# Opening a linear-attention and MLP kernel with a quarter of q loaded by another queue, and with a new order of transposes, sums and products

## Chip, cores and metric

One Trainium2 chip, one NeuronCore. The metric is the device time of one execution in microseconds (us). The kernel before takes 294.88 us, the median of 4 runs (294.63 to 294.96).

The engines, as the profile names them: PE (TensorE matmul), PEld (its weight loads), DVE (VectorE), ACT (ScalarE), POOL (GpSimd) and SP (SyncE, which here only issues DMAs). Each works through its own list of instructions in order and waits on semaphores. DMAs are issued by POOL (all input loads), by SP (output stores, small transfers through DRAM, transposing DMAs) and twice by ACT at the end.

## The reference

```python
# q, k, v: (8, 8, 576, 64) fp32; moe_w_in: (512, 2048); moe_w_out: (2048, 512)
phi = lambda x: np.where(x > 0, x, np.exp(x) - 1.0) + 1.0
q_p, k_p = phi(q), phi(k)
kv  = np.einsum('bhsd,bhse->bhde', k_p, v)
z   = np.sum(k_p, axis=2)
num = np.einsum('bhsd,bhde->bhse', q_p, kv)
den = np.einsum('bhsd,bhd->bhs', q_p, z)[..., None] + 1e-06
x   = (num / den).transpose(0, 2, 1, 3).reshape(4608, 512)
h   = x @ w_in
out = (h - np.tanh(h)) @ w_out
```

## The kernel before

**Layout.** A batch (8 heads of 576 positions) is loaded as four blocks of 128 partitions (8 heads by 64 position groups of J = 9 positions), and held as two halves i = 0, 1. phi (`phi_pieces`, L121) is an exp on ACT (`e`), a max/add on DVE (`r`) and a min on DVE, into `qp` and `kp`. qp is transposed to `qT`: for batches 0 and 1 by PE with copies out of PSUM by ACT or DVE (`a_qT_pe`, L157), for later batches by one transposing DMA on SP (`a_qT_dma`, L151). kv and z come from matmuls of kp with v and with ones (`a_kv` L180, `a_kv_cols` L191 with v repacked by `a_vp` L188; for batch 0 `b0_kv` L216 and `b0_z` L205). DVE multiplies them with a mask of the head blocks into `kz` (L186, L202, L214, L225). `a_den` (L267) multiplies qT with the z columns, DVE takes the reciprocal (L285).

**Spreading 1/den.** For batches 2 and later `a_spread` (L301) writes the reciprocals to DRAM (`ds`, four DMAs on SP) and reads them back on all partitions (`rdb`, two DMAs); `a_num` (L324) multiplies num by rdb into `xT` (L328, L333). For batch 1 the reciprocal is split into bf16 parts (`a_split` L288) and spread by matmuls (`a_spread_pe` L348, line L354), num having been copied from PSUM by ACT (`a_num_copy`, L341); `a_scale` (L359) multiplies. Batch 0 does the same in fp32 (`b0_spread` L235, `b0_num` L227, `b0_scale` L242), with its ninth positions by DRAM (`b0_rest`).

**The MLP.** The 4608 rows go in 9 chunks of 512 (the loop at L502). A chunk does 16 tiles of the first layer (`l1mm`, L366, 4 matmuls each), each pair of tiles followed by tanh on ACT (L372) and a subtraction on DVE (L373) into `gT`, and then 16 steps of 4 matmuls of the second layer (`l2mm`, L387); every fourth step ends a block of 128 rows, copied out by ACT (`evac`, L396) and stored by two DMAs on SP (L401). Chunk 0 has single tiles (`l1act`, L377, L378).

**What sets the order.** It is written out by hand: each engine gets its instructions in the order of the Python calls. Lists `s1[tile]` and `s2[step]` say what of the next batches is put behind which tile or step; this is where the attention work of batch n1 = c + 1 and the phi of batch n2 = c + 2 stand. For chunk 0 s2[3] to s2[15] hold phi of q, transposes, kv, den, num and spread of batch 1, and phi of q and k of batch 2. For chunk 1 kv_cols stands at tile 7 and den at tile 10. From chunk 1 on the loads of batch n2 wait for a small POOL copy (`gate`, L383) of the transposed q of batch n1: they are issued when that transposing DMA has landed.

**The opening** (L404 to L481). POOL issues the two halves of q, of k and of v of batch 0, then the weights and batch 1. PE runs 18 dummy matmuls (`spin`, L444) until the first half of qp is there, transposes it, 5 more, transposes the other half, 6 more, then z(0), kv(0), z(1), den, num(0), kv(1), the spread of two head pairs, num(1). ACT copies three of the four transposed pieces, DVE one. ACT's order is: exp of both q halves, one copy, exp of k half 0, exp of k half 1 in two, two copies, the four small casts `s8` (L460), `sel`, num.

**PSUM.** `ps_all` has 8 banks. The side work of chunk 0 takes banks 4 to 7 in turn, the first layer of later chunks banks 0 to 5, their attention work banks 6 and 7; a matmul that begins a bank waits for whoever last read it.

## Time and profile before

| | us |
|---|---|
| median of 4 runs | 294.88 |
| the profiled execution's own time | 295.09 |
| span of its instructions | 293.3 |
| PE busy | 286.0 |
| DVE busy | 174.7 |
| ACT busy | 139.6 |
| first matmul of the first layer (L366) | 16.70 |
| first layer of chunk 1 begins | 51.26 |
| second layer of chunk 1 begins | 67.25 |

Times in the timeline are from the start of the span. A timeline row is: start, length, engine, line, operation, output and input by the program's names, how many; in brackets the idle time of the engine before it and what ended that. The view of waits has, for each pair of a waiting and a releasing group: total us, times, longest us. Matmuls overlap in PE's pipeline (a 128x512 one shows 379 ns and the next starts 216 ns later), so holes on PE are read from the distance of starts, not from the busy share. A row of the DMA view has 40 equal slices of its window.

### The profile page before, as it was taken

How to read it: one execution, taken by the hardware profiler on the slowest of the kernel's cores; microseconds unless marked ns; L12 is line 12 of the kernel's file. 1: busy time of each engine (PE TensorE's matmuls, PEld its weight loads, DVE VectorE, ACT ScalarE, POOL GpSimd, SP SyncE). 2: the span in 40 equal slices, each digit the busy share in tenths (PEclk: the TensorE clock that was granted, in tenths of full speed). 3: DMA queues.
4: the chain of work that ended last, by engine and by line, in shares of the span. 5: the costliest groups of instructions: out<-in, count | busy, mean ns of one | idle time of the engine just before them, and what ended most of it. 6: DMA issues, size and time to landing. Idle time of an engine off the chain costs nothing.

```text
span 293.3 us, 4504 instructions
## 1 busy us (share of the span) xinstructions
PE 286.0 (98%) x1801; PEld 134.6 (46%) x1801; DVE 174.7 (60%) x265; ACT 139.6 (48%) x168; POOL 33.6 (11%) x55
## 2 busy tenths in 40 slices
PE   8999999999999999999999999999999999999994
PEld 3544453454444444544454444444444444444443
DVE  4759957887467764786478646865581456106600
ACT  4838537947344653455246524661452155126411
POOL 8583030030030003000300020000000000000000
PEclk9999999999999999999999999999999999999999
DMA  6999999998989758945895669767117310131032
GB/s 97 194 204 212 208 207 217 204 146 145 238 162 187 156 118 139 219 119 126 135 223 117 153 134 181 138 151 144 38 23 179 73 36 0 38 84 24 0 74 72
DMA packets 39077, 38.94 MB, mean 133 GB/s; under 512 B 16336, under 2 KB 33808, under 8 KB 38288
## 3 DMA queue, kind: packets, MB, share of 16 engines
q0 software_dynamic: 17552, 18.35, 38.7%
q1 hardware_dynamic: 21344, 20.17, 30.6%
q8 instruction: 14, 0.23, 0.3%
q10 hardware_dynamic: 160, 0.13, 0.1%
q14 instruction: 7, 0.06, 0.0%
HBM read 43.91 MB, written 9.55 MB: 182 GB/s over the span
## 4 chain that ended last, share of the span: by engine, by line
PE 70%; DMA 17%; issue 7%; POOL 2%; DVE 1%; ACT 1%; SPq 1%; POOLq 0%; DVEq 0%
PE ps_all L366 35%; PE ps_all L387 30%; DMA qraw<-in_q_dram 6%; DMA w_in_sb<-in_moe_w_in_dram 3%; DMA rdb<-ds 3%; PE ps_all L199 2%; DMA out_dram<-osb 2%; DMA kraw<-in_k_dram 2%; PE ps_all L317 2%; DMA ds<-rden 1%; PE ps_all L276 1%; ACT osb L396 1%; SPq L401 0%; POOL qraw L90 0%; ACT e L134 0%
## 5 line engine op out<-in xcount | busy, mean ns | idle before, releaser
L366 PE MATMUL ps_all<-xT,w_in_sb 128*128 128x512 bf16 x576 | 128.0, 379 | 0.3 <-DVE xT L244 0.3
L387 PE MATMUL ps_all<-w_out_sb,gT 128*128 128x512 bf16 x560 | 127.8, 379 | 0.0
L373 DVE TENSOR_TENSOR gT<-ps_all,th 128x1024 bf16<-128x1024 f32 x64 | 77.9, 1218 | 59.8 <-ACT th L372 59.8
L372 ACT ACTIVATE th<-ps_all 128x1024 f32<-128x1024 f32 x64 | 65.5, 1024 | 57.0 <-PE ps_all L366 47.1
L366 PEld LDWEIGHTS <-w_in_sb 128*128 128x128 bf16 x576 | 55.3, 98 | 66.6 <-issue 0.6
L387 PEld LDWEIGHTS <-gT 128*128 128x128 bf16 x560 | 54.0, 98 | 64.5 <-issue 0.5
L396 ACT COPY osb<-ps_all 128x512 f32<-128x512 f32 (+1 forms) x36 | 20.9, 582 | 73.7 <-PE ps_all L387 57.3
L328 DVE TENSOR_TENSOR xT<-ps_all,rdb 128x512 bf16<-128x512 f32 x24 | 16.3, 689 | 13.7 <-PE ps_all L317 11.2
L134 ACT ACTIVATE e<-qraw 128x1152 bf16<-128x1152 bf16 x16 | 18.5, 1162 | 6.6 <-DMA qraw<-in_q_dram 6.6
L134 ACT ACTIVATE e<-kraw 128x1152 bf16<-128x1152 bf16 x15 | 17.5, 1165 | 0.2 <-DMA kraw<-in_k_dram 0.2
L136 DVE TENSOR_TENSOR qp<-e,r 128x1152 bf16<-128x1152 bf16 x16 | 12.0, 757 | 7.7 <-ACT e L134 7.2
L136 DVE TENSOR_TENSOR kp<-e,r 128x1152 bf16<-128x1152 bf16 x15 | 11.4, 758 | 8.5 <-ACT e L134 7.6
L383 POOL COPY g<-qT 1x1 bf16<-1x1 bf16 x5 | 1.4, 273 | 120.8 <-DMA qT<-qp 120.8
L378 DVE TENSOR_TENSOR gT<-ps_all,th 128x512 bf16<-128x512 f32 x16 | 10.3, 685 | 2.4 <-ACT th L377 1.7
L377 ACT ACTIVATE th<-ps_all 128x512 f32<-128x512 f32 x16 | 9.2, 598 | 4.3 <-PE ps_all L366 3.1
L444 PE MATMUL ps_all<-zero 128*128 128x512 bf16 x29 | 9.6, 498 | 1.2 <-DVE zero L405 1.2
L317 PE MATMUL ps_all<-qT,kz 128*128 128x512 bf16 x28 | 10.1, 379 | 0.1
L135 DVE TENSOR_SCALAR r<-qraw 128x1152 bf16<-128x1152 bf16 x16 | 7.2, 453 | 2.1 <-DMA qraw<-in_q_dram 2.1
L199 PE MATMUL ps_all<-vp,kp 64*128 64x136 bf16 x216 | 7.4, 220 | 0.4 <-POOL g L383 0.4
L199 PEld LDWEIGHTS <-kp 64*128 64x128 bf16 x216 | 6.4, 94 | 3.0 <-issue 2.1
L285 DVE RECIPROCAL rden<-den 128x144 f32<-128x144 f32 x7 | 7.4, 1053 | 0.2
L394 DVE COPY osb<-ps_all 128x128 f32<-128x128 f32 x1 | 0.3, 290 | 11.6 <-DMA out_dram<-osb 11.6
(82 smaller groups left out, 122.1 us busy)
## 6 DMA issues: line engine op xcount, KB each, us to landing
out_dram<-osb SPq DMA_DIRECT2D x70, 128.0 KB
rdb<-ds SPq DMA_DIRECT2D x12, 576.0 KB
kraw<-in_k_dram POOLq DMA_DIRECT2D x7, 576.0 KB, 7.0
qraw<-in_q_dram POOLq DMA_DIRECT2D x7, 576.0 KB, 9.1
v<-in_v_dram POOLq DMA_DIRECT2D x7, 576.0 KB, 12.1
w_out_sb<-in_moe_w_out_dram POOLq DMA_DIRECT2D x4, 512.0 KB, 16.3
w_in_sb<-in_moe_w_in_dram POOLq DMA_DIRECT2D x6, 256.0 KB, 8.3
qraw<-in_q_dram POOLq DMA_DIRECT2D x2, 288.0 KB, 4.6
```

The lines of the kernel that those rows point to most:

```text
L134: return (lambda: nc.scalar.activation(e, x, AF.Exp), lambda: nc.vector.tensor_scalar(r, x, 0.0, 1.0, ALU.max, ALU.add), lambda: nc.vector ...
L136: lambda: nc.vector.tensor_tensor(y, e, r, ALU.min))
L199: nc.tensor.matmul(ps[hg][:, i, :], kp[r, i, j].rearrange("p h d -> p (h d)"), vp[r, i, j, :], start=(j == 0), stop=(j == J - 1))
L317: nc.tensor.matmul(ps, kz[:, p // 2, p % 2, 0:128], qT[:, p % 2, 0:8, p // 2, :], start=True, stop=True)
L328: nc.vector.tensor_mul(xT[:, p, S * b:S * b + 512].rearrange("p (j t c) -> p j t c", j=8, t=4), ps.rearrange("p j (t c) -> p j t c", t=4), ...
L366: nc.tensor.matmul(h, w_in_sb[:, 2 * (p % 2) + p // 2, fi * 128:(fi + 1) * 128], xT[:, p, c * 512:(c + 1) * 512], start=(n == 0), stop=(n ...
L372: nc.scalar.activation(th, h, AF.Tanh)
L373: nc.vector.tensor_sub(gT[:, fi:fi + 2, :], h, th)
L378: nc.vector.tensor_sub(gT[:, fi, :], h, th)
L387: nc.tensor.matmul(o, gT[:, fi, i * 128:(i + 1) * 128], w_out_sb[:, fi, :], start=(fi == 0), stop=(fi == NF - 1))
L396: nc.scalar.copy(osb[:, f0:f1], o[:, f0:f1])
L444: nc.tensor.matmul(ps_all[:, 0, :], zero[:, 0:128], zero, start=True, stop=True)
```

## The change

Seven edits in one diff, here by place:

- **Load of q, batch 0.** The first half of q was one POOL DMA with two blocks. Now block 0 goes by SP, as fp32, into memory that the pool of `gT` lends (`q_f`); block 1 goes by POOL. POOL's number of DMAs stays the same.
- **phi of that half** is done by block: exp, max/add and min each in two, of 128x576.
- **Order in the opening.** 14, 5 and 5 dummy matmuls instead of 18, 5 and 6. The four casts `s8` stand behind the first two exps. The copies of the transposes stand behind all exps of k: three on ACT, the fourth on DVE behind the mask of z(0). z(1) stands ahead of kv(0); the banks of z and kv are exchanged.
- **Batch 1 in chunk 0.** kv between the two sets of transposes rather than behind both; num right behind den, one step earlier, with the split of the reciprocal.
- **phi of batch 2.** Each piece of q one step later (steps 13, 14, 15 rather than 12, 13, 14), the last beside phi of k.
- **Chunk 1.** exp of k half 1 stays at tile 1, its max/add and min go to tile 3; vp half 1 stays on DVE at tile 3, half 0 goes to ACT at tile 5.
- **Chunk 1.** kv_cols at tile 9 rather than 7, den and its DRAM transfers at tile 11 rather than 10.

On ACT the copies out of PSUM of chunk 0's last two blocks thereby stand one place earlier against the exps, and on SP the transposing DMA of batch 2 stands behind all 8 output stores of chunk 0 rather than behind 6.

```diff
--- before.py
+++ after.py
@@ -87,6 +87,12 @@
         x = src[b].rearrange("h (p j) d -> (h p) (j d)", j=J)
         if halves:
             for i in range(2):
+                if src is q and i == 0:
+
+                    nc.sync.dma_start(out=q_f, in_=x.rearrange("(h i q) x -> h i q x", h=2, i=2)[0, 0])
+                    nc.gpsimd.dma_start(out=t[:, 1, i].rearrange("q j d -> q (j d)"),
+                                        in_=x.rearrange("(h i q) x -> h i q x", h=2, i=2)[1, 0])
+                    continue
                 nc.gpsimd.dma_start(out=t[:, :, i].rearrange("q h j d -> q h (j d)"),
                                     in_=x.rearrange("(h i q) x -> i q h x", h=2, i=2)[i])
         else:
@@ -118,7 +124,7 @@
 
     kp_t, qp_t, qT_t, kz_t, rdb_t, rden_t = {}, {}, {}, {}, {}, {}
 
-    def phi_pieces(b, src, store, name, i, parts=0):
+    def phi_pieces(b, src, store, name, i, xs=None):
 
         if i == 0:
             store[b] = work.tile([128, 2, J, 2, D], BF16, name=name)
@@ -126,11 +132,13 @@
         e = epool.tile([128, 2, J, D], BF16, name="e")
         r = epool.tile([128, 2, J, D], BF16, name="r")
         y = store[b][:, i].rearrange("p j h d -> p h j d")
-        if parts:
-
-            return ([lambda h=h: nc.scalar.activation(e[:, h], x[:, h], AF.Exp) for h in range(2)],
-                    lambda: nc.vector.tensor_scalar(r, x, 0.0, 1.0, ALU.max, ALU.add),
-                    [lambda h=h: nc.vector.tensor_tensor(y[:, h], e[:, h], r[:, h], ALU.min) for h in range(2)])
+        if xs:
+
+            return ([lambda h=h: nc.scalar.activation(e[:, h], xs[h], AF.Exp) for h in range(2)],
+                    [lambda h=h: nc.vector.tensor_scalar(r[:, h], xs[h], 0.0, 1.0, ALU.max, ALU.add)
+                     for h in range(2)],
+                    [lambda h=h: nc.vector.tensor_tensor(y[:, h], e[:, h], r[:, h], ALU.min) for h in range(2)],
+                    lambda: nc.vector.tensor_scalar(r, x, 0.0, 1.0, ALU.max, ALU.add))
         return (lambda: nc.scalar.activation(e, x, AF.Exp),
                 lambda: nc.vector.tensor_scalar(r, x, 0.0, 1.0, ALU.max, ALU.add),
                 lambda: nc.vector.tensor_tensor(y, e, r, ALU.min))
@@ -169,6 +177,18 @@
             else:
                 nc.vector.tensor_copy(dst, src)
 
+    def b0_T(i):
+
+        if i == 0:
+            new_qT(0)
+        src = []
+        for n, (j0, j1) in enumerate(((0, 5), (5, 9))):
+            ps = ps_all[:, 4 + 2 * i + n, :].bitcast(BF16).rearrange("p (j t) -> p j t", t=128)
+            for j in range(j0, j1):
+                nc.tensor.transpose(ps[:, j - j0, :], qp_t[0][:, i, j].rearrange("p h d -> p (h d)"), ident)
+            src.append((qT_t[0][:, i, j0:j1].rearrange("p j g t -> p j (g t)"), ps[:, 0:j1 - j0, :]))
+        return src
+
     def kv_mm(b, i, ps):
         kp, vt = kp_t[b], v_b[b % 2]
         for j in range(J):
@@ -187,6 +207,9 @@
 
     def a_vp(b, i):
         nc.vector.tensor_copy(vp[:, i, :, 0:128].rearrange("p j (h d) -> p h j d", h=2), v_b[b % 2][:, 0:2, i])
+
+    def a_vp_act(b, i):
+        nc.scalar.copy(vp[:, i, :, 0:128].rearrange("p j (h d) -> p h j d", h=2), v_b[b % 2][:, 0:2, i])
 
     def a_kv_cols(b, banks):
         kp = kp_t[b]
@@ -207,22 +230,22 @@
         for j in range(J):
             for hg in range(2):
                 r = slice(64 * hg, 64 * hg + 64)
-                nc.tensor.matmul(ps_all[:, 4 - 2 * i + hg, 0:32], kp_t[0][r, i, j].rearrange("p h d -> p (h d)"),
+                nc.tensor.matmul(ps_all[:, 2 - 2 * i + hg, 0:32], kp_t[0][r, i, j].rearrange("p h d -> p (h d)"),
                                  one[r, 0:32], start=(j == 0), stop=(j == J - 1))
 
     def b0_zc(i):
-        nc.vector.tensor_mul(kz_t[0][:, :, i, 128:160], ps_all[:, 4 - 2 * i:6 - 2 * i, 0:32], mask[:, :, i, 128:160])
+        nc.vector.tensor_mul(kz_t[0][:, :, i, 128:160], ps_all[:, 2 - 2 * i:4 - 2 * i, 0:32], mask[:, :, i, 128:160])
 
     def b0_kv(i):
 
         for j in range(J):
             for hg in range(2):
                 r = slice(64 * hg, 64 * hg + 64)
-                nc.tensor.matmul(ps_all[:, 2 * i + hg, 0:128], kp_t[0][r, i, j].rearrange("p h d -> p (h d)"),
+                nc.tensor.matmul(ps_all[:, 2 + hg, 0:128], kp_t[0][r, i, j].rearrange("p h d -> p (h d)"),
                                  v_b[0][r, 0:2, i, j, :], start=(j == 0), stop=(j == J - 1))
 
     def b0_kz(i):
-        nc.vector.tensor_mul(kz_t[0][:, :, i, 0:128], ps_all[:, 2 * i:2 * i + 2, 0:128], mask[:, :, i, 0:128])
+        nc.vector.tensor_mul(kz_t[0][:, :, i, 0:128], ps_all[:, 2:4, 0:128], mask[:, :, i, 0:128])
 
     def b0_num(i, ns):
 
@@ -405,6 +428,8 @@
     nc.vector.memset(zero, 0.0)
     act0 = rpool.tile([128, 1], F32, name="act0")
     nc.scalar.activation(act0, zero[:, 0:1], AF.Exp)
+
+    q_f = gpool.tile([128, NF, 512], BF16, name="gT").rearrange("p a b -> p (a b)").bitcast(F32)[:, 0:J * D]
     load_q(0)
     load_k(0)
     make_identity(nc, ident)
@@ -445,30 +470,39 @@
 
     side = Banks([4, 5, 6, 7])
     kz_t[0] = kz_c[0]
-    (eq0, rq0, mq0), (eq1, rq1, mq1) = (phi_pieces(0, q_t, qp_t, "qp", i) for i in range(2))
-    for f in (eq0, rq0, mq0, eq1, rq1, mq1):
+    q_h = [q_f.rearrange("p (j d) -> p j d", d=D), q_t[0][:, 1, 0]]
+    eq0, rq0, mq0, _ = phi_pieces(0, q_t, qp_t, "qp", 0, q_h)
+    eq1, rq1, mq1 = phi_pieces(0, q_t, qp_t, "qp", 1)
+    eq0[0]()
+    rq0[0]()
+    eq0[1]()
+
+    for t in range(4):
+        nc.scalar.copy(s8[32 * t:32 * t + 32, 0].rearrange("q h p -> q (h p)"),
+                       ident[32 * t:32 * t + 32, 32 * t:32 * t + 8])
+    for f in (rq0[1], *mq0, eq1, rq1, mq1):
         f()
-    spin(18)
-    a_qT_pe(0, 0, side, "AV")
-    (ek0, rk0, mk0), (ek1, rk1, mk1) = (phi_pieces(0, k_t, kp_t, "kp", i, 2 * i) for i in range(2))
+    spin(14)
+    T0 = b0_T(0)
+    ek0, rk0, mk0 = phi_pieces(0, k_t, kp_t, "kp", 0)
+    ek1, _, mk1, rk1 = phi_pieces(0, k_t, kp_t, "kp", 1, [k_t[0][:, h, 1] for h in range(2)])
     for f in (ek0, rk0, *ek1, mk0, rk1):
         f()
     spin(5)
-    a_qT_pe(0, 1, side, "AA")
-
-    for t in range(4):
-        nc.scalar.copy(s8[32 * t:32 * t + 32, 0].rearrange("q h p -> q (h p)"),
-                       ident[32 * t:32 * t + 32, 32 * t:32 * t + 8])
+    T1 = b0_T(1)
+    for x in (*T0, T1[0]):
+        nc.scalar.copy(*x)
     nc.scalar.copy(sel, s8[:, 0].rearrange("q h p -> q p h").unsqueeze(3).to_broadcast([128, NP, 2, 64]))
-    spin(6)
+    spin(5)
     b0_z(0)
     for f in mk1:
         f()
     b0_zc(0)
+    b0_z(1)
+    nc.vector.tensor_copy(*T1[1])
+    b0_zc(1)
     b0_kv(0)
     b0_kz(0)
-    b0_z(1)
-    b0_zc(1)
     a_den(0, Banks([4]))
     ns0 = new_ns(0)
     b0_rest()
@@ -523,10 +557,9 @@
             s2[3].append(lambda: a_qphi(1, 0))
             s2[4].append(lambda: (a_qphi(1, 1), load_q(2), load_k(2), load_v(2)))
             s2[0].append(prepare)
-            s2[7].append(lambda: (a_qT_pe(1, 0, side), a_qT_pe(1, 1, side), a_kv(1, side)))
+            s2[7].append(lambda: (a_qT_pe(1, 0, side), a_kv(1, side), a_qT_pe(1, 1, side)))
             s2[8].append(lambda: b0_scale_rest(side))
-            s2[9].append(lambda: a_den(1, side))
-            s2[10].append(lambda: (num1(), a_split(1)))
+            s2[9].append(lambda: (a_den(1, side), num1(), a_split(1)))
             s2[11].append(lambda: spread1(0))
 
             def q2(n):
@@ -540,19 +573,19 @@
                         x[2]()
                     a_qT_dma(2)
 
-            s2[12].append(lambda: q2(0))
-            s2[13].append(lambda: (spread1(1), q2(1)))
-            s2[14].append(lambda: q2(2))
-            s2[15].append(lambda: a_kphi(2, 0))
+            s2[13].append(lambda: (spread1(1), q2(0)))
+            s2[14].append(lambda: q2(1))
+            s2[15].append(lambda: (q2(2), a_kphi(2, 0)))
         elif n1 < B:
-            s1[7 if c == 1 else 5].append(lambda: a_kv_cols(n1, attn))
-            s1[10 if c == 1 else 8].append(lambda: (a_den(n1, attn), a_spread(n1)))
+            s1[9 if c == 1 else 5].append(lambda: a_kv_cols(n1, attn))
+            s1[11 if c == 1 else 8].append(lambda: (a_den(n1, attn), a_spread(n1)))
             for p in range(NP + 1):
                 s2[(11 if c == 1 else 9) + p].append(lambda p=p: a_num(n1, p))
         if c == 1:
-            s1[1].append(lambda: a_kphi(2, 1))
-            for i in range(2):
-                s1[3].append(lambda i=i: a_vp(2, i))
+            k21 = phi_pieces(2, k_t, kp_t, "kp", 1)
+            s1[1].append(k21[0])
+            s1[3].append(lambda: (k21[1](), k21[2](), a_vp(2, 1)))
+            s1[5].append(lambda: a_vp_act(2, 0))
         if c >= 1 and n2 < B:
 
             s1[0].append(lambda: (gate(qT_t[n1]), load_k(n2), load_q(n2), load_v(n2)))
```

## Prediction

> **What bounds the kernel.** I first read busy time and granted clock on the page.
>
> ```profile
> span 293.3 us, 4504 instructions
> ...
> PE 286.0 (98%) x1801; PEld 134.6 (46%) x1801; DVE 174.7 (60%) x265; ACT 139.6 (48%) x168; POOL 33.6 (11%) x55
> ...
> PEclk9999999999999999999999999999999999999999
> ```
>
> PE is the bound, at full clock. No PE work worth counting is added or removed, so the change can only move PE's late start and its few holes. Next I read who PE waited for:
>
> ```profile
> PE ps_all L354 <- ACT ns L344: 0.7, 1, 0.7
> PE ps_all L221 <- DMA v<-in_v_dram: 0.4, 1, 0.4
> PE ps_all L199 <- POOL g L383: 0.4, 1, 0.4
> PE ps_all L366 <- DVE xT L244: 0.3, 1, 0.3
> PE ps_all L164 <- DVE qp L136: 0.2, 1, 0.2
> ```
>
> A releaser here is the semaphore that came last: L199 names a GpSimd copy, but PEld beside it was held by the vp copies (L189). From the starts of single matmuls in the timeline, less 512 columns at 0.216 us, the holes after 17 us are: 0.37 at 38.7 (L164), 0.86 at 46.1 (L354), 0.53 at 57.9 (L199), 0.27 at 79.55 (L317, not listed above). After 80 us there is none. So the prize is 2.0 us plus whatever the first layer (L366, at 16.70) starts earlier.
>
> Third, the opening's timeline:
>
> ```profile
> 10.79 1.26 ACT L131 ACTIVATE e<-kraw 128x576 bf16<-128x576 bf16 x2 [0.32 <-DMA kraw<-in_k_dram]
> 11.95 1.16 ACT L168 COPY qT<-ps_all 128x640 bf16<-128x640 bf16 x2
> 12.21 0.68 PE L221 MATMUL ps_all<-v,kp 64*128 64x128 bf16 x18 [0.41 <-DMA v<-in_v_dram]
> 12.71 0.40 PE L210 MATMUL ps_all<-one,kp 64*128 64x32 bf16 x18
> 13.90 1.06 DVE L285 RECIPROCAL rden<-ps_all 128x144 f32<-128x144 f32 x1 [0.42 <-PE ps_all L276]
> 16.70 0.59 PE L366 MATMUL ps_all<-xT,w_in_sb 128*128 128x512 bf16 x2 [0.33 <-DVE xT L244]
> ```
>
> The halves land one after another (q 5.6 and 7.0, k 9.3 and 10.7, v 12.2): v lands, then kv(0), z(1), zc, den, reciprocal, spread, scale, L366.
>
> Fourth, the hole at 79.55, by the DMA and SP views of 64 to 80 us (0.4 us a slice):
>
> ```profile
> GB/s 213 202 213 204 213 207 205 202 213 202 213 206 209 206 56 0 0 0 0 184 161 92 253 184 115 230 138 346 300 207 253 115 246 143 236 318 381 341 244 133
> ```
>
> ```profile
> 65.41 1.28 SPq L305 DMA_DIRECT2D ds<-rden  x4
> 70.61 1.12 SPq L308 DMA_DIRECT2D rdb<-ds  x2
> ```
>
> The four small ds stores wait behind the loads of batch 3, which end at 69.9; rdb is issued only then, its data begins at 71.6 and has landed at 79.2, and L328 starts at 79.29. PE resumes at 80.03. So time won before 80 us counts only as far as rdb of batch 2 also lands earlier.
>
> **The change, part by part.**
>
> *Opening: the load.* A quarter of q goes by SyncE; the GpSimd queue carries that much less. Halves follow each other 1.40 us apart (5.6 to 7.0; k 9.3 to 10.7), so the quarter is 0.70. The page's DMA row is near empty until GpSimd's first packets at 2.78, and the two 0.62 us slices after that run at 35 and 33 GB/s against some 200: there is room. Let s be how much earlier all later halves land. Ends: below nothing, -0.35, if the quarter runs beside GpSimd's packets and its fp32 writes (twice the bytes) cost half a quarter; above, 1.4, if it also takes the slow first 0.7 us upon itself. I take 0.70. The trace has no unloaded load by SyncE: rdb's first data came 1.0 us after its issue, so with an issue near 0.75 the quarter's data starts near 1.8 and lands near 3.5, outer bound 5.6 as now.
>
> The Trainium skill ("DMA: Bandwidth & Descriptors", section "Rules for kernel authors") speaks against this part: spreading DMAs over issuing engines does not help bandwidth, since all run on the same 16 DMA engines. By it s is 0 and the start is 0.18 us later; the trace shows those engines idle before 2.78, a case the rule does not treat, so I go by the trace.
>
> Exp and max/add become two of half size: 0.68 each on ACT (L131 row) against 1.16, and 0.23 to 0.69 on DVE (half of the bf16 row; the 128x512 fp32 rows of L378). They are covered: the transposes cannot start before 14 spins end at about 7.2 (14 x 0.43 from 1.19).
>
> *Opening: the order.* ACT now has exp of k half 1, starting 0.09 after it lands (10.79 - s), then three copies, then part two of den. Starts in the trace are 0.59 apart for an exp, 0.57 for a 640 copy, 0.48 for a 512 copy; the last copy (640) takes 0.67. So the third copy ends at 10.79 + 2 x 0.59 (11.95) + 0.57 + 0.48 + 0.67 = 13.67 - s. PE: z(1) follows the last min (ends 12.56) at 12.72 - s, takes 0.24; kv(0) 0.50; eps and den part one 0.17: ready at 13.63 - s. Den's second part starts at 13.72 - s against 13.54 now; the reciprocal keeps its 0.36 behind that: 14.08 - s against 13.90. DVE's mask of kv starts at 13.68 - s, frees DVE at 14.02 - s, just in time. Everything after keeps its distance (ns and the second mask are ready before the spread). **First layer earlier by s - 0.18 = 0.52.**
>
> *Batch 1.* PE now does 9 transposes (0.50), 36 kv (1.60), 9 transposes (0.50) = 2.60 where it took 41.33 - 38.26 = 3.07: +0.47. Cover: v of batch 1 must have landed (38.74 now, 38.04 then; kv at 38.23). If that cover goes, the hole returns as a wait on v.
>
> *num beside den, spread later.* After den (43.27 now) w is ready 3.23 later, the copies that free the banks 3.02, PE arrives 3.09 later. So the 0.86 hole shrinks to about 0.24, what is late being w: +0.62. Lead at the first layer of chunk 1: 0.52 + 0.47 + 0.62 = 1.61.
>
> *Chunk 1.* ACT: the exps of q and k batch 2 stand one evacuation later, so the first tanh starts 1.2 earlier instead of 1.61; the vp copy costs ACT about 1.16 (the 128x1152 exp row) and spares DVE 0.37. kv_cols two tiles later finds vp ready: the 0.53 hole goes. But DVE now does max/add, min, vp and the subtractions of tiles 4 to 9 (1.13 apart) before the masks: masks end at 62.38, den on PE is wanted at 61.32: a new hole of 1.1, and 0.15 at tile 8. Lead left behind den: 0.99.
>
> *rdb of batch 2.* The reciprocal ends at 65.13 against 65.38 (0.25 earlier, held by tanh and subtraction of tiles 10 and 11). The transposing DMA that opens the loads of batch 3 goes behind 8 output stores rather than 6, at 52.75 against 53.43 (53.43 is right behind the sixth store; then the eighth, as the last evacuation ends 1.2 earlier). So the loads end 0.68 earlier. ds ends with whichever is later: issue plus 4.2 (65.41 to 69.6) moves 0.25, end of the loads moves 0.68. In chunk 2 ds took only 1.5 (issued 94.30, as its loads ended), so I take the end of the loads. L328 and PE's return move from 80.03 to 79.35; the other 0.3 of lead is waited away there.
>
> **Sum:** 0.68 against the profiled execution's own 295.09 (span 293.3), which stands 0.21 above the median 294.88. I forecast **294.2** by the median.
>
> **Rivals.**
> A, the forecast, 45%: gain 0.25 (ds keeps its own delay) to 0.9, at 0.68.
> B, more, 22%: s near 1.4, because SyncE's packets also take the slow start; then the first layer is 1.2 earlier and rdb with it: some 1.3, **293.6**. For: the two slow slices. Against: the slowness may be GpSimd's queue's own.
> C, the quarter is not free, 20%: s is 0, first layer 0.18 later. Batch 1's and num's gains stay but are waited away at 80, because the loads' end does not move for the better: 0.0 (-0.4 to +0.2), **294.9**. This is also the case where the change doesn't do what it says. Against: idle DMA engines.
> D, slower, 13%: the transposing DMA of batch 2 is late. Its place is SP's queue behind two more stores (1.31 us of issue now behind it). If ACT's last evacuation of chunk 0 does not end earlier than now (52.67), issue is 0.5 later and the stores' data, 0.5 us, goes ahead: loads, ds, rdb and PE's return are all 1.0 later: **295.9**. It decides from a gate copy (POOL L383, 58.22) that starts later than now. For: PE's slack there is nil. Against: PE brings 1.61 of lead.
>
> **Numbers.** 0.2%, 0.59 us, is about what a measurement of this kernel can tell from no change. Of A some six tenths lie beyond it. Faster: 22 + 27 = 49%; same: 18 of A + 19 of C = 37%; slower: 13 + 1 = 14%. The range reaches to 293.3 (below B's middle) and 295.7 (most of D outside): about 15% is left out.
>
> **What would show it.** Right: exp of k half 1 near 10.1; reciprocal near 13.4; L366 near 16.2; no wait at the batch-1 transposes; spread waiting under 0.3; a new wait of den on DVE kz near 61; gate copy near 57.5; PE back at about 79.4. Wrong: a quarter landing after 4.5 or halves not earlier (C); kv waiting for v near 38; the gate copy after 58.2 (D); or no wait at rdb although it lands no earlier, which would break the step that everything before 80 us is measured by rdb.

## The result and the profile after

| | before | after |
|---|---|---|
| median | 294.90 (56 runs) | 295.56 (38 runs) |
| ratio after / before, 95% interval | | 1.0022 [1.0017, 1.0027] |
| the profiled execution's own time | 295.09 | 296.13 |
| span of its instructions | 293.3 | 294.4 |
| first matmul of the first layer | 16.70 | 17.05 |
| first layer of chunk 1 begins | 51.26 | 51.01 |
| reciprocal of batch 2 ends | 65.38 | 66.57 |
| first rdb DMA of batch 2 issued | 70.61 | 71.79 |
| PE back at num of batch 2 | 80.03 | 81.10 |

The change costs 0.66 us, 0.22%, where 0.68 was forecast as a gain. The profiled execution of after is 0.57 slower than its median, that of before 0.19, so the 1.1 us between the two traces is 0.4 more than what the medians say. One execution of the kernel e10 below ran in a slower state (304.08 us) and is left out of its median, 293.55; the text recorded ahead of e14 has 293.66, with it.

The page of after, busy time, and the view of PE's waits (waiting group, releasing group: total us, times, longest us):

```profile
span 294.4 us, 4495 instructions
...
PE 284.1 (97%) x1796; PEld 133.5 (45%) x1796; DVE 175.2 (60%) x266; ACT 140.6 (48%) x170; POOL 33.6 (11%) x55
```

```profile
PE ps_all L340 <- DVE xT L351: 0.9, 1, 0.9
...
PE ps_all L299 <- DVE kz L225: 0.5, 1, 0.5
PE ps_all L389 <- DVE xT L267: 0.3, 1, 0.3
PE ps_all L410 <- DMA w_out_sb<-in_moe_w_out_dram: 0.2, 1, 0.2
```

The lines are those of after: L389 is before's L366 (first layer), L410 the second layer, L340 and L351 num and its product with rdb (before L317, L328), L299 den, L308 the reciprocal, L377 the spread. Set against before, three waits are gone from the view: of the spread for ns (0.7), of kv_cols (0.4) and of the batch-1 transposes (0.2). Three stand in their place: den waits for kz, the second layer waits for a piece of w_out, and num waits for rdb nearly four times as long as before (1.03 against 0.27). By starts of single matmuls less 512 columns at 0.216 us the holes are 0.40 at 41.3 (w_out), 0.20 at 46.6 (spread), 0.14 at 57.7, 0.66 and 0.28 at 62.6 and 63.5 (den), 1.03 at 79.9 (num). From 81 us on there is none, as before.

The opening of after (start, length, engine, line, operation, output and input, how many; in brackets the idle time before it and its end):

```profile
3.69 0.68 ACT L137 ACTIVATE e<-gT 128x576 bf16<-128x576 f32 x1 [1.45 <-DMA gT<-in_q_dram]
...
10.86 1.26 ACT L137 ACTIVATE e<-kraw 128x576 bf16<-128x576 bf16 x2 [0.31 <-DMA kraw<-in_k_dram]
...
12.02 1.75 ACT L494 COPY qT<-ps_all 128x640 bf16<-128x640 bf16 x3
...
14.25 1.06 DVE L308 RECIPROCAL rden<-ps_all 128x144 f32<-128x144 f32 x1 [0.18 <-PE ps_all L299]
...
17.05 0.59 PE L389 MATMUL ps_all<-xT,w_in_sb 128*128 128x512 bf16 x2 [0.33 <-DVE xT L267]
```

The quarter landed at 3.66, close to the 3.5 forecast. (The 14 dummy matmuls ended at 5.8, not at the 7.2 of the forecast: they start 0.43 apart until 4.0 and 0.22 apart after it, while in before the change comes at 7.0. No later step hung on it.) But exp of k half 1 starts at 10.86, where 10.79 stood before and 10.1 was forecast: the later halves came no earlier. Every DMA of GpSimd lands on 16 DMA engines, each with a mark of its own in the trace. Last marks, before to after: q half 1 6.99 to 7.87, k 9.28 to 9.36 and 10.70 to 10.77, v 12.17 to 12.17. First marks: 6.61 to 5.76, 8.16 to 7.46, 9.85 to 9.07, 11.37 to 10.54. So the first engine does come 0.7 to 0.85 earlier, and the last, for which the consumer waits, does not.

The bytes that the DMA engines moved in the first 16 us, 0.4 us a slice, before and then after:

```profile
GB/s 0 0 0 0 0 0 9 52 23 118 213 207 202 204 216 196 147 141 184 207 190 202 164 193 193 199 210 190 216 196 213 182 174 178 192 193 191 195 200 214
```

```profile
GB/s 0 0 0 0 69 167 300 242 190 159 95 89 167 156 158 161 181 173 182 196 181 170 199 205 173 207 190 225 196 205 183 198 188 194 195 192 200 202 202 200
```

After moves data 1.0 us sooner (first packets at 1.78 and 2.78), then drops to 89 to 95 GB/s at 4.0 to 4.8 and stays near 160 until 6.4, where before is at 196 to 216.

The way to rdb of batch 2 in after, on DVE and then by SyncE's queue (both parts cut to the rows in question), with the bytes of 64 to 80 us (0.4 us a slice):

```profile
62.96 0.78 DVE L225 TENSOR_TENSOR kz<-ps_all,mask 128x272 bf16<-128x272 f32 x2
64.04 1.22 DVE L396 TENSOR_TENSOR gT<-ps_all,th 128x1024 bf16<-128x1024 f32 x1 [0.30 <-ACT th L395]
65.19 0.30 DVE L304 TENSOR_SCALAR den<-ps_all 128x144 f32<-128x144 f32 x1
65.52 1.05 DVE L308 RECIPROCAL rden<-den 128x144 f32<-128x144 f32 x1
```

```profile
66.60 1.29 SPq L328 DMA_DIRECT2D ds<-rden  x4
71.79 1.12 SPq L331 DMA_DIRECT2D rdb<-ds  x2
```

```profile
GB/s 237 190 202 207 207 207 210 204 205 207 210 207 210 204 206 186 45 13 14 0 0 0 184 161 276 276 69 207 161 254 230 300 207 184 230 143 182 256 379 365
```

den's addition on DVE stands behind one subtraction of tanh (L396), as before; all of it is 1.19 later. ds to rdb takes 5.19, before it took 5.20; rdb to the product 8.57, before 8.67. What is lost at the reciprocal, 1.19, arrives at num but for 0.1 (1.07).

### The profile page after: what moved, and what is told of

Its sections match the earlier page's. It is cut to its first block, busy times and chain, and to the rows that moved or that the text cites. A ratio compares the mean times of both kernels' runs of the same rounds, so it can differ in the third digit from the quotient of the medians.

```text
span 294.4 us, 4495 instructions
## 1 busy us (share of the span) xinstructions
PE 284.1 (97%) x1796; PEld 133.5 (45%) x1796; DVE 175.2 (60%) x266; ACT 140.6 (48%) x170; POOL 33.6 (11%) x55
## 4 chain that ended last, share of the span: by engine, by line
PE 78%; DMA 16%; POOL 2%; issue 1%; DVE 1%; SPq 0%; ACT 0%; DVEq 0%; POOLq 0%
PE ps_all L389 37%; PE ps_all L410 35%; DMA w_out_sb<-in_moe_w_out_dram 6%; DMA w_in_sb<-in_moe_w_in_dram 3%; DMA rdb<-ds 3%; DMA kraw<-in_k_dram 3%; PE ps_all L222 2%; PE ps_all L340 2%; DMA ds<-rden 1%; PE ps_all L637 1%; PE ps_all L299 1%; POOL v L444 1%; DVE rden L308 0%; PE ps_all L343 0%; ACT th L395 0%
## 5 line engine op out<-in xcount | busy, mean ns | idle before, releaser
L389 PE MATMUL ps_all<-xT,w_in_sb 128*128 128x512 bf16 x576 | 128.2, 379 | 0.3 <-DVE xT L267 0.3
L410 PE MATMUL ps_all<-w_out_sb,gT 128*128 128x512 bf16 x560 | 127.6, 379 | 0.2 <-DMA w_out_sb<-in_moe_w_out_dram 0.2
L396 DVE TENSOR_TENSOR gT<-ps_all,th 128x1024 bf16<-128x1024 f32 x64 | 77.9, 1219 | 60.1 <-ACT th L395 60.1
L389 PEld LDWEIGHTS <-w_in_sb 128*128 128x128 bf16 x576 | 55.2, 98 | 66.8 <-issue 0.9
L410 PEld LDWEIGHTS <-gT 128*128 128x128 bf16 x560 | 54.2, 98 | 65.6 <-issue 1.5
L351 DVE TENSOR_TENSOR xT<-ps_all,rdb 128x512 bf16<-128x512 f32 x24 | 16.3, 689 | 14.4 <-PE ps_all L340 11.2
L142 ACT ACTIVATE e<-qraw 128x1152 bf16<-128x1152 bf16 x15 | 17.3, 1162 | 4.4 <-DMA qraw<-in_q_dram 4.4
L144 DVE TENSOR_TENSOR qp<-e,r 128x1152 bf16<-128x1152 bf16 x15 | 11.4, 757 | 7.7 <-ACT e L142 7.0
L340 PE MATMUL ps_all<-qT,kz 128*128 128x512 bf16 x28 | 10.1, 379 | 0.9 <-DVE xT L351 0.9
L469 PE MATMUL ps_all<-zero 128*128 128x512 bf16 x24 | 7.1, 448 | 1.2 <-DVE zero L428 1.2
L308 DVE RECIPROCAL rden<-den 128x144 f32<-128x144 f32 x7 | 7.4, 1053 | 0.2
```

The lines of the kernel that those rows point to most:

```text
L142: return (lambda: nc.scalar.activation(e, x, AF.Exp), lambda: nc.vector.tensor_scalar(r, x, 0.0, 1.0, ALU.max, ALU.add), lambda: nc.vector ...
L144: lambda: nc.vector.tensor_tensor(y, e, r, ALU.min))
L340: nc.tensor.matmul(ps, kz[:, p // 2, p % 2, 0:128], qT[:, p % 2, 0:8, p // 2, :], start=True, stop=True)
L351: nc.vector.tensor_mul(xT[:, p, S * b:S * b + 512].rearrange("p (j t c) -> p j t c", j=8, t=4), ps.rearrange("p j (t c) -> p j t c", t=4), ...
L389: nc.tensor.matmul(h, w_in_sb[:, 2 * (p % 2) + p // 2, fi * 128:(fi + 1) * 128], xT[:, p, c * 512:(c + 1) * 512], start=(n == 0), stop=(n ...
L396: nc.vector.tensor_sub(gT[:, fi:fi + 2, :], h, th)
```

## The experiments

Theory 1: the loss is made in chunk 1, where den's later place puts the reciprocal, and with it ds and rdb of batch 2, behind PE's need. Theory 2: the quarter sets the 16 DMA engines apart, and all later landings carry it. Rival to both: the new order of the opening. Ratios are to the kernel before, run beside each (its medians there: 294.86 to 295.06), with 95% intervals.

| kernel | us | ratio |
|---|---|---|
| after | 295.56 | 1.0022 [1.0017, 1.0027] |
| e1: after without the quarter | 295.44 | 1.0010 [1.0001, 1.0018] |
| e2: the quarter alone | 295.29 | 1.0007 [0.9998, 1.0015] |
| e3: after, chunk 1 and q of batch 2 as before | 294.54 | 0.9990 [0.9975, 1.0004] |
| e4: batch 1's two edits alone | 294.14 | 0.9971 [0.9960, 0.9982] |
| e5: e4 and the opening's order | 294.36 | 0.9979 [0.9970, 0.9987] |
| e6: e4 and chunk 1's edits | 295.23 | 1.0008 [0.9999, 1.0017] |
| e7: e4 and q of batch 2 one step later | 294.89 | 0.9996 [0.9987, 1.0005] |
| e8: e4, w_out's third piece ahead of v | 298.17 | 1.0111 [1.0095, 1.0126] |
| e9: e4 and kv_cols at tile 8 | 294.08 | 0.9973 [0.9964, 0.9983] |
| e10: e9 and that piece in two DMAs | 293.55 | 0.9955 [0.9942, 0.9968] |
| e11: q half 0 as two quarters by GpSimd | 297.01 | 1.0063 [1.0045, 1.0080] |
| e12: e9 and the quarter | 294.83 | 0.9997 [0.9982, 1.0011] |
| e13: e4, kv_cols and den at tiles 9 and 11 only | 294.92 | 1.0005 [0.9994, 1.0015] |
| e14: e10, v of batch 3 after rdb of batch 2 | 293.59 | 0.9961 [0.9947, 0.9976] |

**e1, without the quarter.** From after:

```diff
-                if src is q and i == 0:
-                    nc.sync.dma_start(out=q_f, in_=x.rearrange("(h i q) x -> h i q x", h=2, i=2)[0, 0])
-                    ...
-    eq0, rq0, mq0, _ = phi_pieces(0, q_t, qp_t, "qp", 0, q_h)
-    eq1, rq1, mq1 = phi_pieces(0, q_t, qp_t, "qp", 1)
+    (eq0, rq0, mq0), (eq1, rq1, mq1) = (phi_pieces(0, q_t, qp_t, "qp", i) for i in range(2))
```

> The changed kernel with its first half of q loaded whole by GpSimd and its phi done whole, as before; everything else of the change stays. Theory 1 (the loss is made behind the opening: den of batch 2 comes later, so its reciprocals are spread later and PE stands before 80 us; the quarter itself is nearly neutral, because the slowest of the 16 DMA engines lands no earlier with it): first layer near 16.9 (0.18 later than before for the copies on ACT), halves of q, k, v landing as before, PE back at the num of batch 2 between 80.4 and 81.1, time 295.1 to 295.6, still slower than before. Theory 2 (the quarter by SyncE sets the 16 DMA engines apart and so makes every later load end later): the spread between first and last engine is again 1 us at most, the w_out wait near 41.7 goes, rdb lands as before or earlier, time 294.3 to 294.8.

Still slower than before. The first layer starts at 16.84, the spread waits 0.21, den 0.66 and 0.28, the reciprocal ends at 66.00 and num waits 0.88. There is no wait for w_out. So a loss is made without the quarter. How much of after's 0.22% it is, the intervals don't say well: 0.01 to 0.18% here.

**e2, the quarter alone**, with phi of that half by blocks, in the kernel before.

> The kernel before with only the quarter of q by SyncE as fp32 and the phi of that half by blocks. Theory 1: within 0.1% of before, 294.7 to 295.2; first layer at 16.7 to 16.8; the last DMA engine lands k and v within 0.15 us of before. Theory 2: 295.3 to 296, with the weights w_out and the loads of batch 3 ending 0.4 to 1.7 us later than before and PE waiting for them at 41 and for rdb at 80. Theory 3 (the edits in chunk 1 make the loss): 294.9.

Last engines: k 9.54 and 10.95, v 12.36, each 0.2 to 0.3 later than before; first layer at 16.89. Its runs lie between 294.34 and 295.69, more than a microsecond apart; by the interval the quarter alone neither gains nor loses.

**e3, chunk 1 undone.** From after:

```diff
-            s2[13].append(lambda: (spread1(1), q2(0)))
-            ...
+            s2[12].append(lambda: q2(0))
+            ...
-            s1[9 if c == 1 else 5].append(lambda: a_kv_cols(n1, attn))
-            s1[11 if c == 1 else 8].append(lambda: (a_den(n1, attn), a_spread(n1)))
+            s1[7 if c == 1 else 5].append(lambda: a_kv_cols(n1, attn))
+            s1[10 if c == 1 else 8].append(lambda: (a_den(n1, attn), a_spread(n1)))
```

> The changed kernel with chunk 1 as before: kv_cols at tile 7, den and its transfers at tile 10, vp twice on DVE, phi of k half 1 at tile 1, and phi of q of batch 2 at steps 12, 13, 14 again. Theory 1 and theory 3 (the edits in chunk 1 make the loss): the reciprocal of batch 2 ends near 65.2, as PE enters chunk 1 0.25 earlier than before, ds is issued about 1.2 earlier than in the changed kernel, PE returns from the rdb wait between 79.7 and 80.2, time 294.5 to 295.0. Theory 2 (the quarter by SyncE delays all later loads): little changes, 295.3 to 295.7, since the loads of batch 3 still end 1 us or more later than before.

294.54: undoing chunk 1 takes 1.0 us off. In this profile the quarter did win: last engines k 8.69 and 10.11, v 11.56, and a first layer at 16.39. Its other runs reach up to 295.64, so that is not the rule. The last section comes back to this scatter.

**e4, batch 1 alone.** From before:

```diff
-            s2[7].append(lambda: (a_qT_pe(1, 0, side), a_qT_pe(1, 1, side), a_kv(1, side)))
+            s2[7].append(lambda: (a_qT_pe(1, 0, side), a_kv(1, side), a_qT_pe(1, 1, side)))
-            s2[9].append(lambda: a_den(1, side))
-            s2[10].append(lambda: (num1(), a_split(1)))
+            s2[9].append(lambda: (a_den(1, side), num1(), a_split(1)))
```

> The kernel before with only the batch 1 edits of chunk 0: kv between the two sets of transposes and num right behind den. The hole ahead of the spread shrinks from 0.86 to 0.25; the hole at the transposes goes, but the next second-layer step waits for w_out (landed 41.26 before) and gives that back. PE enters chunk 1 0.6 earlier. Theory 1: the lead counts only as far as the reciprocal of batch 2 and rdb come earlier; the reciprocal is held by DVE in chunk 1, so 0.1 to 0.5 remains, 294.4 to 294.8. Theory 2 says the same of it, as there is no quarter: 294.3 to 294.5 if rdb follows in full.

The edits at one of the seven places gain 0.29%; those at the other six take it back. PE's waits in e4:

```profile
PE ps_all L199 <- POOL g L383: 0.4, 1, 0.4
PE ps_all L366 <- DVE xT L244: 0.3, 1, 0.3
PE ps_all L387 <- DMA w_out_sb<-in_moe_w_out_dram: 0.2, 1, 0.2
```

The wait at num of batch 2 is not there. The hole of the spread is 0.20. A new hole of 0.41 stands at 41.3, where before none was: the third piece of w_out has landed on its last engine at 41.27 here and at 41.26 before, and PE came to it at 41.33 before. The swap of kv and transposes won its time and PE waited it away at once.

**e5, e6, e7: the other edits on top of e4.** e5 is after without the quarter and with e3's undoing. e6 adds to e4 tiles 9 and 11 and the pieces of phi and vp:

```diff
-            s1[1].append(lambda: a_kphi(2, 1))
-            for i in range(2):
-                s1[3].append(lambda i=i: a_vp(2, i))
+            k21 = phi_pieces(2, k_t, kp_t, "kp", 1)
+            s1[1].append(k21[0])
+            s1[3].append(lambda: (k21[1](), k21[2](), a_vp(2, 1)))
+            s1[5].append(lambda: a_vp_act(2, 0))
```

e7 adds the later steps of q2 alone.

> The kernel before with batch 1's kv between its transposes and num beside den (the edits of the run of them alone: 294.14 us, ratio 0.9971), plus the new order of the opening (copies on ScalarE behind all exps of k, z ahead of kv); q whole by GpSimd, chunk 1 as before. Theory 1 (the loss sits in chunk 1's later den): the order costs only the 0.2 to 0.3 us by which the first layer starts later: first matmul of the first layer near 16.8 to 16.85, rdb of batch 2 lands 0.2 to 0.3 later than in that run (78.13), no wait at num of batch 2 over 0.1; time 294.35 to 294.45, ratio 0.998. Rival (the order of the opening carries what the run without the quarter lost, 295.44): ratio 1.001, 295.2 or more. Rival that the order is free: 294.15.

294.36: the order costs 0.2, with intervals that overlap, and the first layer starts at 16.71 against e4's 16.57. As theory 1 had it, but for a hole of 0.33 at num, where at most 0.1 was expected.

> The kernel before with batch 1's two edits (294.14 us, 0.9971 alone) plus chunk 1's edits without the later steps of q of batch 2: kv_cols at tile 9, den at 11, phi of k in pieces, one vp on ScalarE. No quarter, opening as before. Theory 1: the wait of kv_cols (0.54) goes, den waits some 0.66 and 0.28 for VectorE, batch 2's reciprocal ends about 1.2 us later than in that run (64.71, so near 65.9), rdb lands as much later (near 79.3) and PE waits at num of batch 2 about 0.8; time 294.9 to 295.1, ratio near 1.000. Rival (the opening order or the loads carry the loss): rdb no later than PE's need, 294.1 to 294.2.

295.23: chunk 1's edits cost 1.1 on top of e4. The reciprocal ends at 66.59, and num waits 0.57. Of the 1.88 by which the reciprocal ends later than in e4, 0.59 was there when chunk 1 began (51.17 against 50.57): in this profile the opening's loads are late, though nothing of them was changed (k half 0's last engine at 9.57, the first layer at 16.99).

> The kernel before with batch 1's two edits (294.14 us) plus only the pieces of q of batch 2 one step later, so that its transposing DMA stands behind two more stores on SyncE. Rival D of the prediction: the transposing DMA 0.6 us later (near 53.35 instead of 52.75), the gate copy and the loads of batch 3 0.6 later, and by the prediction's choice (ds moves with the end of the loads) rdb 0.6 later: a small wait at num, 294.3 to 294.6. Theory 1 (ds's own delay of about 4.1 us from its issue governs, not the end of the loads): gate 0.6 later, ds and rdb unmoved within 0.2, time 294.1 to 294.2.

294.89: 0.75, more than either side expected. The transposing DMA went from 52.75 to 53.66 and the gate from 57.54 to 58.43. But most of the cost came by another way: the later pieces of q push vp back on DVE, kv_cols waits 0.91 rather than 0.54, and the reciprocal ends 0.42 later. The rest of the 0.68 by which num resumes later lies behind it: ds takes 5.27 from its issue to its last landing, 5.08 in e4. The wait of kv_cols in the view:

```profile
PE ps_all L199 <- DVE vp L189: 0.7, 1, 0.7
```

The two are not additive: from e5 to e1 both are added, for 1.08 together. With kv_cols at tile 9 its wait for vp is gone anyway.

**e8, w_out ahead of v.** `load_wo(2)` and `load_v(1)` change places in e4.

> The kernel before with batch 1's two edits (294.14 us) plus the third piece of w_out loaded ahead of v of batch 1. If the 0.41 wait of the second layer's tile 8 at 41.3 is for the landing of that piece, it goes and v of batch 1 lands later instead, by the piece's own time; v then ends kv's wait. Theory: w_out's wait 0.41 to 0, kv of batch 1 waits 0.2 to 1.5 more than its 0.18 (the piece is as large as a load of v); net -0.3 to +1.0, likeliest a loss near +0.5, 294.6. If the hole is not for w_out, 0.41 stays and kv waits too.

The hole at w_out goes, so it was for that piece. But kv now waits 2.86 for v, more than was allowed for: 298.17. The wait itself explains 2.3 of the 4.0 over e4 (2.86 less the 0.18 and 0.41 that go). The rest is PE's clock: 0.5 us after this wait the granted clock falls to 0.5 for 3.4 us (41.6 to 45.0), which is an estimated 1.7 us. The page's row of the clock, with the rows of all other kernels but e11 at 9 throughout:

```profile
PEclk9999989999999999999999999999999999999999
```

**e9, kv_cols at tile 8**, den staying at tile 10, on e4.

> The kernel before with batch 1's two edits (294.14 us alone, ratio 0.9971), and kv_cols of batch 2 at tile 8 of chunk 1 instead of 7, den kept at tile 10; nothing else of the change. Theory 1 (what counts in chunk 1 is when batch 2's reciprocal ends; ds and rdb follow it at fixed distances of 5.1 and 8.2 to 8.5 us): PE reaches tile 8 at 58.1, vp is ready at 57.96 to 58.33, so the 0.54 wait goes; kv ends near 59.2, VectorE's kz as now at 60.5 to 61.3, den's slot on PE at 61.35, just behind it; den, the reciprocal (64.71) and rdb (78.13) are all up to 0.54 earlier, with num following: time 293.6 to 293.9, ratio 0.995 to 0.996. Rival (VectorE, not PE, sets the reciprocal, as with den at tile 11): kv_cols' wait goes but den waits for kz or the reciprocal stays at 64.7; PE comes 0.5 earlier to num and waits there: 294.1.

The rival came nearer: 294.08 against 294.14. The two can't be told apart by their intervals. The wait of kv_cols is gone, but the reciprocal ends only 0.25 earlier (64.46), and rdb's product starts at 78.10 against 78.22.

**e10, the piece of w_out in two.** On e9:

```diff
-    load_wo(2)
+    for r in (1024, 1280):
+        nc.gpsimd.dma_start(out=w_out_sb[:, r // 128:r // 128 + 2, :],
+                            in_=moe_w_out[r:r + 256, :].rearrange("(ko ki) f -> ki ko f", ki=128))
```

> As the run with kv_cols at tile 8, and the third piece of w_out loaded as two DMAs of half the size, in the same place of GpSimd's queue, so that the second layer's tile 8 needs only the first of them. If the 0.41 wait at 41.3 is for the landing of that piece's last engine, it goes (the first half lands near 40.3), and everything behind it is 0.3 to 0.4 earlier: 293.3 to 293.6. Rival: rdb of batch 2 is what PE meets next and does not come earlier by as much, or the extra issue on GpSimd (about 1 us) delays the fourth piece: no gain, 293.7 to 294.0.

293.55, 0.45% below before. The first half lands at 40.23, and the second layer no longer waits. PE is then early enough to meet rdb again, with 0.44 at num by the starts of its matmuls (the view of waits gives 0.3):

```profile
PE ps_all L317 <- DVE xT L328: 0.3, 1, 0.3
```

**e11, two quarters by GpSimd**, in the kernel before: the cut of the load without SyncE and without fp32.

> The kernel before with q half 0 loaded as two quarters, both by GpSimd in bf16, and phi of q half 0 by blocks: the split without SyncE and without fp32. Compare with the run of the SyncE quarter alone (last engine of k half 1 at 10.95, of v half 1 at 14.03, first-to-last spread 1.3 to 2.1; 1.0007). Theory 2 (a load on a second queue sets the 16 DMA engines apart): the spread of each landing is as before (0.4 to 1.1), k half 1 lands at 10.7 to 10.9, the time is within 0.1% of before (one more issue costs up to 0.2). Rival (the split, or chance, does it): spread over 1.3 here too.

The rival: the spread from first to last engine is 2.29 for q half 1 and 2.2 for k, and k's last engines are at 10.31 and 11.70, 1.0 later than before. The first layer waits until 18.87, 2.2 later, and the landings are only half of that. q half 1, on its last engine at 8.84 rather than 6.99, leaves PE without work for 2.19, and then the clock falls as in e8, to 0.5 from 11.8 to 15.2. The page's row of the clock and two rows of the timeline:

```profile
PEclk9799999999999999999999999999999999999999
10.87 0.68 PE L174 MATMUL ps_all<-ident,qp 128*128 128x128 bf16 x9 [2.19 <-DVE qp L146]
18.87 0.38 PE L376 MATMUL ps_all<-xT,w_in_sb 128*128 128x512 bf16 x1 [0.33 <-DVE xT L254]
```

So theory 2 in its form (a second queue) falls: the engines come apart without SyncE too. Of the 2 us that e11 costs in time, a part is this clock.

**e12, the quarter on e9.**

> As the run with kv_cols at tile 8, plus the SyncE quarter and phi of q half 0 by blocks, with the opening order of before. The prediction's step (later halves land 0.7 earlier, everything up to rdb follows): 0.5 to 0.7 less than that run. Theory 1 (the last engine lands no earlier): first matmul of the first layer within 0.3 of 16.7, time 0 to 0.3 us more than that run and a wider scatter of its runs. A landing of k half 1 before 10.3 would be a second case like the run with chunk 1 undone (10.11), and would show that it varies from run to run.

294.83, and runs from 293.79 to 296.21, where e9's lie within 0.7. In the profile the last engines are at 9.80 (k), 11.22 and 12.65 (v), and the first layer starts at 17.18, 0.95 later than in e9. At chunk 1 only 0.11 of that is left: e9 had waited 0.41 for v of batch 1 and 0.41 for w_out, and e12 does not. The opening's lead is waited away at 38 to 41 us as long as the loads do not come earlier too.

**e13, the tiles alone**, and **e14, one load taken from beside ds.** What was open was which part of chunk 1 costs, and by what rdb moves. e14 changes e10:

```diff
-            s1[0].append(lambda: (gate(qT_t[n1]), load_k(n2), load_q(n2), load_v(n2)))
+            if c == 1:
+                s1[0].append(lambda: (gate(qT_t[n1]), load_k(n2), load_q(n2)))
+                def late_v():
+                    g1 = rpool.tile([1, 1], F32, name="g1")
+                    nc.gpsimd.tensor_copy(g1, rdb_t[2][0:1, 0, 0, 0, 0:1])
+                    load_v(3)
+                s1[12].append(late_v)
```

> The kernel before with batch 1's two edits (294.14 us), plus kv_cols of batch 2 at tile 9 and den at tile 11 of chunk 1; phi of k and both vp on VectorE as before (without the pieces of the run with chunk 1's edits added, 295.23 us). Theory 1a (den's tile is what costs): batch 2's reciprocal ends 1.2 to 1.4 later than 64.71, near 66.0; gate copy unmoved near 57.5; over the runs so far rdb's issue is well fitted by 8.72 + 0.40 x gate copy + 0.59 x ds issue, which gives 70.7 here; PE waits some 0.4 to 0.5 at num of batch 2; time 294.6 to 294.9. Rival 1b (the pieces make VectorE's backlog, the tiles cost nothing): reciprocal near 65.2, 294.2 to 294.4. For ds's own delay alone rdb's issue would be 71.2, for the end of the loads alone 69.9.

294.92, the reciprocal at 66.28: theory 1a. The tiles cost 0.8 of e6's 1.1 by the medians, 1.0 by the ratios. DVE's kz is at 61.9 and den's addition at 64.89, where e4 has 63.32. num waits longer than the 0.4 to 0.5 expected, because rdb is issued at 71.21, not 70.7:

```profile
PE ps_all L317 <- DVE xT L328: 1.3, 1, 1.3
```

> As the run with w_out's third piece split (293.66 us), and in chunk 1 v of batch 3 is loaded only when rdb of batch 2 has landed (a copy of one element of rdb on GpSimd ahead of it), so that two loads, not three, run beside ds. Theory S (ds shares the DMA engines with the loads that are in flight, and lands about when they end): k and q end near 65.9, rdb's issue near 67 to 67.7 instead of 69.8, rdb landed before 76.5, no wait of PE at num of batch 2 (0.44 there); time 293.1 to 293.4. Rival O (ds has its own delay of 5.1 to 5.6 from its issue): rdb's issue 69.4 to 69.8, wait 0.3 to 0.44, 293.5 to 293.7. Rival L (v lands too late for vp of batch 3 in the second layer of chunk 1): PE waits at chunk 2, over 294.

ds has landed at 67.11 instead of 69.71, and PE no longer waits at num:

```profile
64.19 1.29 SPq L305 DMA_DIRECT2D ds<-rden  x4
67.23 1.12 SPq L308 DMA_DIRECT2D rdb<-ds  x2
```

```profile
GB/s 213 204 210 204 162 32 14 3 0 0 0 230 323 184 230 276 253 184 346 115 276 300 69 218 154 277 195 81 52 112 179 170 150 150 138 124 189 294 287 226
```

The stream of the loads thins out from 65.6 on (the row is that of 64 to 80 us again), and rdb is issued 3.04 after ds, in e10 5.56. Theory S holds for ds: it is the traffic beside it that makes it late. Its time, 293.1 to 293.4, was not reached: 293.59 is no lower than e10's 293.55. The wait of 0.44 is gone from the profile, but the medians don't show it. v of batch 3 lands at 80.7, and PE has no hole behind that.

**Taken together.** e4 stands at -0.29%; the order brings it to -0.21% (e5), chunk 1 with the later q to +0.10% (e1), the quarter to +0.22% (after). Theory 1 names the largest of the three losses, 0.31% of the 0.51%, and the only one whose two intervals lie clear of each other; the order (0.08%) and the quarter (0.12%) carry the rest, each with intervals that overlap. In e3 and e12 a good part of the quarter's cost is a granted clock that falls in some executions (last section): at a mean clock of 0.998 and more their medians are 294.28 and 294.43, no worse than e5's 294.36 for e3, and 0.35 above e9 for e12. In after it matters little: without the four of 38 executions concerned the median is 295.51.

## Why the prediction was wrong, point by point

**PE is the bound, holes are the prize: right.** The sum of holes went from 2.0 to 2.7, and the first layer started 0.35 later; the trace's 1.1 us is these two. PE's return at num was forecast at 79.35 and came at 81.10. Nearly all of these 1.75 is two terms, worked out below: 1.36 of lead that chunk 1 never got, and 0.43 (0.68 less 0.25) of the wrong choice at rdb.

**Opening, the load: wrong, and the step that cost most of the forecast.** s was taken as 0.70. By the last engines of k and v half 0 it was -0.1 to 0.0 in after, -0.25 in e2, -0.5 in e12, and only in e3 0.6. The failed reason is "the GpSimd queue carries that much less": true for the first engine, not for the last. The landing estimate itself (3.5; 3.66 measured) was good. Where s was 0.6, in e3's profile, the lead did come: chunk 1 begins at 49.91 there, 1.35 earlier than before. The Trainium skill ("DMA: Bandwidth & Descriptors", section "Rules for kernel authors") had said that spreading DMAs over issuing engines does not help bandwidth; I set it aside for the idle engines. The last landings of after, e2 and e12 agree with the rule, those of e3 do not.

**Opening, the order: right, but a tenth too small.** 0.18 was forecast. From the last landing of k half 1 to the first layer it is 6.00 in before and 6.28 in each of the four profiles with the new order (after, e1, e3, e5), so the order costs 0.28. Den's second part starts 0.21 later by this measure, as forecast within 0.03; the reciprocal then follows it by 0.43 rather than the 0.36 that was to be kept.

**Batch 1: the cover was misnamed.** The forecast let the +0.47 stand unless v was late. PE's next need was w_out's third piece, on time to 0.07 us before the change. With the first layer's 0.35 and a last engine that is 0.45 later (41.71), batch 1 gave -0.07 instead of +0.47. The forecast had v as the only cover; the second landing was a term that it put at nothing.

**num beside den: right.** 0.86 to 0.24 was forecast, 0.86 to 0.20 measured. It is nearly e4's whole gain in lead (51.26 to 50.57, 0.69).

So the lead at chunk 1 was 0.25 instead of 1.61: 0.87 lost in the opening, 0.54 in batch 1.

**Chunk 1: right in its holes, and the lead is missing again.** A den hole of 1.1 and 0.15 at tile 8 were forecast, 0.94 and 0.14 measured. The reciprocal was to end at 65.13 and ended at 66.57: 1.44, of which 1.36 is the missing lead. The profiles bear that out, since the reciprocal keeps its distance to chunk 1's own start: 14.1 in before, e2, e3, e4, e5, e8 and e11 (den at tile 10), 13.9 in e9, e10, e12 and e14 (kv_cols at tile 8), 15.4 to 15.6 in after, e1, e6 and e13 (den at tile 11), and 14.5 in e7. The forecast had 15.48. So it had the price of the later den right, and paid it with lead that never came.

**rdb of batch 2: the wrong one of two.** I had ds end with whichever is *later*, its own delay or the end of the loads. For the first landing it is whichever comes *earlier*; the last follows it by 0.9 to 1.7. (The 1.5 that the forecast read for ds in chunk 2 does not come out of the trace: the first mark there is 1.12 behind the issue, the last 2.23.) Issue, first landing and last of ds, eight of the 16 profiles:

| kernel | ds issued | first lands after | v's load, first engine | ds all landed |
|---|---|---|---|---|
| before | 65.41 | 3.85 | 69.84 | 70.50 |
| after | 66.60 | 3.85 | 70.47 | 71.65 |
| e4 | 64.74 | 3.89 | 69.13 | 69.82 |
| e7 | 65.15 | 3.85 | 70.05 | 70.42 |
| e10 | 64.26 | 3.94 | 69.09 | 69.71 |
| e6 | 66.61 | 3.35 | 69.79 | 71.09 |
| e13 | 66.31 | 3.06 | 69.17 | 71.09 |
| e14 | 64.19 | 2.02 | 66.04 (q) | 67.11 |

While loads run, ds's first mark comes 3.84 to 3.94 after the issue in 13 of 16 profiles, whether v's first engine lands 0.02 or 1.04 us behind that. In the other three (e6, e13, e14) the load ends sooner, and ds's first mark stands 0.17 to 0.19 behind it. So a reciprocal that is 0.25 earlier would have brought PE back an estimated 0.25 earlier, not 0.68. With the 1.36 of lead that is all: 80.03 - 0.25 + 1.36 = 81.14, measured 81.10.

**The rivals.** C had the opening right (s = 0) but not its end, since it kept batch 1's gain. D's sign was seen (gate copy at 58.87, later than 58.22), and the time is near its 295.9, but that is luck, for its mechanism is not shown: the loads' median engine ended 0.56 later, while ds kept its own 3.85 from the issue, and e7 costs more than half of its 0.75 by way of DVE and kv_cols. What the forecast lacked is a rival in which the lead fails and den is late all the same.

## What to carry to other kernels

A lead that an early stage wins counts only up to the next load that is just in time: list the landings that PE meets with no slack (here v and w_out at 38 to 41 us) before adding leads up. A step put later because a lead will pay for it is a bet on that lead; here den one tile and kv_cols two tiles later cost 0.8 to 1.0 us by themselves, and batch 1's two edits, which needed no lead, gave 0.29% alone. When a consumer waits for a DMA, read the landing of its last engine, not its first, and for a small DMA behind large ones ask what it stands behind. When runs of one kernel scatter, set their times against their granted clock first: here a wait of PE of over 2 us cost an estimated 1.7 more.

## What the hardware showed that I had not expected

- A small DMA by SyncE beside three running GpSimd loads needs 3.85 us to its first landing, and 2.02 when the loads end in the meantime (e14); in chunk 2 of before, where one engine of the last load is still to land, it needs 1.12. The Trainium skill ("DMA: Bandwidth & Descriptors", section "Queues, rings and completion order") says that a DMA engine takes turns between queues, a packet of some 9 to 17 descriptors at a time. At the 0.11 us that a record of the loads takes here, and if a record is a descriptor, that would be an estimated 1.0 to 1.9 us; the 3.85 measured is longer, and the measurement decides.
- With q's first load cut into two transfers of 128 rows the engines lie further apart in four of five profiles: 1.5 to 2.2 us from first to last mark for the halves of k and v (e11 without SyncE; after, e2 and e12 with it), against 0.8 to 1.1 in before. In after it still shows at 41 us (39.05 to 41.71). That the cut is the cause is likely, but one profile a kernel does not show it: in the uncut kernels the same spread runs from 0.4 (e9) to 1.2 (e14) and in e6 to 1.5, and e3's, with the cut, drew together again (0.66 by k half 1). Why is not settled.
- PE's clock follows its waits. In the profiles of e8 and e11 a wait of PE of 2.7 and of 2.2 us is followed, 0.5 and 1.0 us after PE resumes, by 3.4 us at half the granted clock; after a wait of 1.65 us (after, at 8.25) the clock stays at 1.0, and no other profile has such a stretch before its last microseconds. One such stretch makes a mean clock of 0.994, and runs of 0.992 to 0.994 occur only in e8 (4 of 4) and in kernels with the cut load: e11 (3 of 6), e3 (4 of 12, at 295.36 to 295.64, while the other eight take 293.55 to 294.59), e12 (3 of 12, its slowest), after (4 of 38). So part of the wider scatter with the quarter (294.81 to 296.68 in after, 293.79 to 296.21 in e12, against 294.57 to 295.37 before) is likely the opening's wait for q crossing some length between 1.65 and 2.2 us; the runs themselves were not profiled.
- In e13 seven of the eight engines that ds's last DMA lands on were done at 70.14 and the eighth at 71.09. One packet of instruction code falls into the stretch (the DMA view of 62 to 73 us counts one, of 0.02 MB). With kv_cols at tile 7 that packet starts within 2.2 us of the gate copy, or 3.1 in e3, and v's last engine is 0.02 to 0.63 behind the 15th; with kv_cols at tile 8 or 9 it starts 3.6 to 6.0 behind the gate, and the last engine (q's in e14) is 0.65 to 0.94 behind, so the two groups nearly touch. That a moved block of matmuls moves a code load into the loads fits all 16 profiles, but it was not tried by itself.
